# Attention and two expert layers in one kernel: plain loads of q and k with rounding on engines, and another order of batches

## The chip, the cores and the metric

One core of a Trainium2 chip runs the whole program. The time is in microseconds of the device, from the start to the end of one execution. The kernel before had 793.51 us as the median of 3 runs (792.83 to 797.36). One further execution was recorded by the profiler, and all rows below come from it.

## What is computed

Three parts follow each other. Attention over 4 batches of 8 heads, 576 positions, 64 columns a head, with a causal mask and a bias from running sums; then an expert layer that takes the largest of three projections; then an expert layer that sends each of the 2304 tokens to one of 8 experts.

```python
def _attn_ref(q, k, v, s) -> np.ndarray:
    ...
    s_pos = np.maximum(s, 0.0)
    cum = np.cumsum(s_pos, axis=-1)
    bias = -(cum[:, :, :, None] - cum[:, :, None, :])
    scores = np.where(causal, -1000000000.0, scores + np.minimum(bias, 0.0))
    ...
    return np.matmul(attn, v).astype(np.float32)
...
    h = np.maximum(np.maximum(x @ w1, x @ w2), x @ w3)
    return (h @ w_out).astype(np.float32)
...
    e_idx = np.argmax(logits, axis=1)
    ...
        h = np.maximum(x[mask] @ w1[e], 0.0)
        out[mask] = gate_w[mask, None] * (h @ w2[e])
```

## The kernel before

**Precision.** An fp32 value is held as a rounded part of type fp32r ("hi", the names `hl`, `xh`, `w_h`) and what is left of it ("lo", `xl`, `w_l`). A product of two such values takes three matmuls on PE (TensorE): hi by hi, lo by hi, hi by lo. Somebody has to round, and somebody has to subtract.

**Attention.** The 16 pairs of heads `p` are worked through two heads at a time, 32 heads in all. `load(p, j)` brings in a head. Before, it makes three transfers of q and k from memory: SP's queue loads `qk_r` (q in partitions 0 to 63, k in 64 to 127, 288 KB), and POOL's queue loads with a cast to fp32r into `hl` (k's hi of 64x576, 144 KB, L191; q twice, 128x576, 288 KB, L192). Then `k_b`, k's hi once more, comes by a casting load for p < 2 (L194) or from `hl` by a copy on SP's queue, 144 KB. `split` makes the lo parts: k's on DVE into `hl` (L210), q's on POOL into `q_b` (L211). `scores` does two matmuls for each of six blocks (L239, L240), DVE adds the mask and takes the least value (L241), ACT takes the exponential (L243). `inverse` handles the sums (L254), `turned` transposes on PE (L272) with copies on DVE (L275) and ACT (L277), and `values_of` multiplies with v (L295) and writes the result into `x`, scaled by DVE (L296, L297). `load` runs L_AHEAD heads ahead and `split` one head ahead of `scores`.

**Work put between heads.** As soon as all four pairs of a batch are done, projections of the first expert layer for its tokens are put between the heads of later batches (`fill`, with `xh` cast by ACT at L308 and `xl` by POOL at L309): NFILL[b] of the six groups `f`, in pieces of 288 tokens, through PSUM pool `ps_f` and the DRAM array `h_d`. `convert` turns the weights into hi and lo parts (L120 on ACT, L122 and L123 on DVE, L127 on ACT, L128 on POOL); those of `f` < 3 during attention, the fifteen others behind it (`rest`).

**Behind attention.** Six windows of 384 tokens, in the order of the tokens. `stage_a` does the groups `f` that were not done ahead (36 matmuls each, L141 to L143: 4 blocks of 3 for each of three weights), `stage_b` the out-projection of 128 tokens (18 matmuls, L549 to L551), `route` the gating, eight DVE operations a tile (L479) and a ranking on PE (L488). Then the experts run in units of 256 tokens; the weights of the first units are made during the last windows (L591, L592).

**What sets the order.** Each engine works through its list in order. A scheduler that estimates times fixes the lists when the program is built; `issue_after` and `high_priority` bind some instructions to others. SP's and POOL's queues of transfers run in the order of issue.

Of the kernel before, what the change touches and what calls it, by code (L numbers as in the profile page):

```python
# [5 lines left out]
F32 = mybir.dt.float32  # L6
F32R = mybir.dt.float32r
BF16 = mybir.dt.bfloat16
I32 = mybir.dt.int32
ALU = mybir.AluOpType  # L10
# [5 lines left out]
B, H, S, D = 4, 8, 576, 64  # L16
# [6 lines left out]
NP = B * H // 2  # L23
# [29 lines left out]
SENT = 1 << 20  # L53
TABLE = E * STRIDE + UNIT

NFILL = [2, 3, 2, 0]
NPRE = 3
FW = S // 2
FILL_0 = 2
# [7 lines left out]
Z_BUFS = 2  # L67
W1_BUFS = 18
PT_BUFS = 10
L_AHEAD = 4  # L70
FILL_N = [9, 8, 6]
PSB = (3, 3, 1, 1)
HL_BUFS = 4
QR_BUFS = 3
KB_BUFS = 4
QB_N = 3
S_AHEAD = 1
E_N = 4
# [5 lines left out]
def fused_kernel(tc, qk, vd, sd, w64, mod, wg, wgt, mb, we, cst, csi, out):  # L84
    nc = tc.nc
    V, A, G, P, SP = nc.vector, nc.scalar, nc.gpsimd, nc.tensor, nc.sync
    top = ExitStack()
    with top:
# [58 lines left out]
        with ExitStack() as es:  # L147
# [35 lines left out]
            last_load = [None]  # L183


            def load(p, j):
                hl = qkp.tile([128, 2, S], F32R, name="hl", bufs=HL_BUFS)
                x = qkp.tile([128, S], F32, name="qk_r", bufs=QR_BUFS)
                k_b = qkp.tile([66, S], F32R, name="k_b", bufs=KB_BUFS)
                SP.dma_start(out=x, in_=qk[p, :, 0, j])  # L190
                G.dma_start(out=hl[64:128, 0], in_=qk[p, 64:128, 0, j])  # L191
                G.dma_start(out=hl[:, 1], in_=qk[p, :, 1, j])  # L192
                if p < 2:
                    G.dma_start(out=k_b[0:64], in_=qk[p, 64:128, 0, j])  # L194
                if p == 0:
                    A.dma_start(out=k_b.bitcast(F32)[64:66], in_=augk.bitcast(F32)[16 * j:16 * j + 1])
                    if j == 0:
                        SP.dma_start(out=mask[:, S - 128:S], in_=cst[:, 256:384])
                        SP.dma_start(out=ident, in_=cst[:, 0:128])
                else:  # L200
                    if p > 1:
                        SP.dma_start(out=k_b.bitcast(F32)[0:64], in_=hl.bitcast(F32)[64:128, 0])
                    last_load[0] = SP.dma_start(out=k_b.bitcast(F32)[64:66], in_=dk[p, :, j]).ins
                return p, j, hl, x, k_b


            def split(t):
                p, j, hl, x, k_b = t
                q_b = qbs[(2 * p + j) % len(qbs)]
                V.tensor_tensor(out=hl[0:64, 0], in0=x[64:128], in1=hl.bitcast(F32)[64:128, 0], op=ALU.subtract)  # L210
                ins = G.tensor_tensor(out=q_b[0:64], in0=x[0:64], in1=hl.bitcast(F32)[0:64, 1], op=ALU.subtract).ins  # L211
                return ins, (hl, q_b, k_b)

            def values_in(p):
                v_r = vp.tile([128, 5, 128], F32, name="v_r")
                SP.dma_start(out=v_r, in_=vd[p])
                return v_r

            def scores(j, qkb):
# [61 lines left out]


            def values_of(p, v_r, rb, pts):
                b, hp = divmod(p, H // 2)
                if hp == 0:
                    xb[b] = xbp.tile([128, DM // 128, S], F32, tag="xb", name=f"x{b}")
                o_0 = ps_t.tile([128, 512], F32, name="t_ps")
                o_ps = ps_o.tile([128, 512], F32, name="o_ps")

                ins = last_t[0]  # L290
                with tc.high_priority():
                    for o, a0, kb, (i, a, n) in [(o_ps, 512 - t[2], kb, t) for kb, t in enumerate(PV)] + [(o_0, 0, 0, (2, 256, 64))]:
                        for j in (1, 0):
                            with tc.issue_after(ins):
                                ins = P.matmul(o[j * 64:(j + 1) * 64, a0:a0 + n], v_r[:, kb, j * 64:(j + 1) * 64], pts[j][i][:, a:a + n], start=kb == 0, stop=kb == len(PV) - 1 or o is o_0).ins  # L295
                V.tensor_tensor(out=xb[b][:, hp, 64:S], in0=o_ps, in1=rb[:, 128:640], op=ALU.mult)  # L296
                V.tensor_tensor(out=xb[b][:, hp, 0:64], in0=o_0[:, 0:64], in1=rb[:, 64:128], op=ALU.mult)  # L297
# [99 lines left out]
            for p in range(1, NP):  # L397
# [15 lines left out]
                    with tc.issue_after(exps[-1 - CONV_LAG]), tc.issue_after(last_load[0]):  # L413
                        convert(n // 3, n % 3, w0p, "w0", rawp, early=True)
                if p % (H // 2) == H // 2 - 1:
                    b = p // (H // 2)
                    n = 0
                    for i in range(b * S // FW, (b + 1) * S // FW if NFILL[b] else 0):
                        xx, hs = [], {}
                        todo.append((n_head + FILL_0 + n * FILL_N[b] / (6 * NFILL[b]), lambda i=i, xx=xx: xx.extend(fill_x(i, fxp, "fx", V if XL_V else G))))  # L420
                        for f in range(NFILL[b]):
                            for j in range(3):
                                todo.append((n_head + FILL_0 + n * FILL_N[b] / (6 * NFILL[b]), lambda i=i, f=f, j=j, xx=xx, hs=hs: fill(i, f, j, xx, hs, ps_f, fhp, "fh")))
                                n += 1
# [411 lines left out]
def _layout(i):  # L836
# [3 lines left out]
        return a.reshape(NP, 2, S, D).transpose(0, 3, 1, 2)  # L840

    q, k = heads(i["q"]), heads(i["k"])
    qk = np.stack([np.concatenate([q, k], axis=1), np.concatenate([q, q], axis=1)], axis=2)
    v = i["v"].reshape(NP, 2, S, D).transpose(0, 2, 1, 3).reshape(NP, S, 2 * D)
    vd = np.concatenate([v, np.zeros((NP, 64, 2 * D), np.float32)], axis=1).reshape(NP, 5, 128, 2 * D).transpose(0, 2, 1, 3)
    s = i["s"].reshape(NP, 2, S).transpose(1, 0, 2).reshape(2 * NP, S)
# [37 lines left out]
```

## Time and profile before

| | |
|---|---|
| median of 3 runs | 793.51 us |
| profiled execution, its own time | 789.03 us |
| its span | 787.2 us |
| TensorE's mean granted clock | 0.979 |
| PE busy | 722.2 us, 92% |
| DVE busy | 561.1 us, 71% |
| POOL busy | 390.5 us, 50% |
| ACT busy | 361.6 us, 46% |
| DMA read and written | 98.85 and 12.18 MB |

The span is the time between the first and the last instruction that the profiler saw, and the profiled execution's own time holds it. Attention takes the first 285 us, the windows of the first layer end at about 560 us, and the rest are the experts' units. The share of busy time is a mean over these.

### The profile page before, as it was taken

How to read it: one execution, taken by the hardware profiler on the slowest of the kernel's cores; microseconds unless marked ns; L12 is line 12 of the kernel's file. 1: busy time of each engine (PE TensorE's matmuls, PEld its weight loads, DVE VectorE, ACT ScalarE, POOL GpSimd, SP SyncE). 2: the span in 40 equal slices, each digit the busy share in tenths (PEclk: the TensorE clock that was granted, in tenths of full speed). 3: DMA queues.
4: the chain of work that ended last, by engine and by line, in shares of the span. 5: the costliest groups of instructions: out<-in, count | busy, mean ns of one | idle time of the engine just before them, and what ended most of it. 6: DMA issues, size and time to landing. Idle time of an engine off the chain costs nothing. (4 is left out here: it accounts for less than half of the span.)

```text
span 787.2 us, 13802 instructions
## 1 busy us (share of the span) xinstructions
PE 722.2 (92%) x4566; PEld 639.7 (81%) x4566; DVE 561.1 (71%) x1475; ACT 361.6 (46%) x908; POOL 390.5 (50%) x413
## 2 busy tenths in 40 slices
PE   2588699989999995999999999989999999999996
PEld 1566478768988884999989899988998889998884
DVE  5688698879777557876989485983576778666740
ACT  3375456555656444522222222334554655656541
POOL 6544536463433045635263433367456777856641
PEclk9998999999999998999999999999999999999999
DMA  8979768779662156210120101337734766857520
GB/s 196 208 216 229 197 181 200 195 213 247 186 174 80 43 188 193 91 56 21 51 48 17 36 15 52 123 80 219 253 105 164 252 216 242 271 197 251 189 83 18
DMA packets 50706, 118.01 MB, mean 150 GB/s; under 512 B 10497, under 2 KB 14497, under 8 KB 50625
## 3 DMA queue, kind: packets, MB, share of 16 engines
q1 hardware_dynamic: 38216, 90.45, 37.0%
q0 software_dynamic: 12400, 26.57, 13.2%
q8 instruction: 38, 0.62, 0.4%
q14 instruction: 44, 0.35, 0.2%
q10 hardware_dynamic: 8, 0.01, 0.0%
HBM read 98.85 MB, written 12.18 MB: 141 GB/s over the span
## 5 line engine op out<-in xcount | busy, mean ns | idle before, releaser
L141 PE MATMUL a_ps<-xh,w_h 128*128 128x384 f32 (+2 forms) x492 | 159.0, 325 | 3.4 <-DVE h L320 2.9
L142 PE MATMUL a_ps<-xl,w_h 128*128 128x384 f32 (+2 forms) x492 | 158.6, 323 | 0.0
L143 PE MATMUL a_ps<-xh,w_l 128*128 128x384 f32 (+2 forms) x492 | 157.0, 320 | 0.0
L592 DVE TENSOR_TENSOR e_l<-e_raw,e_h 128x512 fp32r<-128x512 f32 x80 | 106.9, 1345 | 43.1 <-ACT e_h L591 40.9
L592 POOL TENSOR_TENSOR e_l<-e_raw,e_h 128x512 fp32r<-128x512 f32 x80 | 109.1, 1383 | 39.4 <-ACT e_h L591 35.0
L243 ACT ACTIVATE e<-e,mn 128x64 f32<-128x64 f32 (+4 forms) x160 | 89.1, 558 | 85.2 <-DVE mn L241 84.8
L479 DVE CUSTOM_DVE_ANT_0 junk<-x,wg 128x512 bf16<-128x512 f32 x120 | 96.4, 804 | 31.8 <-ACT x L553 30.4
L591 ACT CAST e_h<-e_raw 128x512 fp32r<-128x512 f32 x160 | 93.3, 621 | 50.6 <-DMA e_raw<-in_we 38.7
L141 PEld LDWEIGHTS a_ps<-xh,w_h 128*128 128x128 f32 x492 | 93.3, 190 | 5.5 <-DVE h L320 3.7
L142 PEld LDWEIGHTS a_ps<-xl,w_h 128*128 128x128 f32 x492 | 93.6, 190 | 0.9
L143 PEld LDWEIGHTS a_ps<-xh,w_l 128*128 128x128 f32 x492 | 93.5, 190 | 0.5
L239 PE MATMUL s_ps<-hl 128*128 128x64 f32 (+2 forms) x192 | 66.7, 360 | 23.4 <-DMA hl<-in_qk 10.8
L622 PE MATMUL h_ps<-x2t,e_h 128*128 128x256 f32 x288 | 81.0, 286 | 1.1 <-DVE gl L628 1.1
L272 PE MATMUL t_ps<-ident,e 128*128 128x128 f32 x480 | 71.8, 285 | 10.5 <-ACT r_t L259 5.1
L625 PE MATMUL h_ps<-x2t,e_h 128*128 128x256 f32 x288 | 81.0, 283 | 0.0
L626 PE MATMUL h_ps<-x2t,e_l 128*128 128x256 f32 x288 | 80.9, 282 | 0.0
L540 POOL TENSOR_TENSOR fl<-h,fh 128x384 fp32r<-128x384 f32 x36 | 42.8, 1194 | 73.9 <-ACT fh L539 51.7
L241 DVE CUSTOM_DVE_ANT_0 e<-s_ps,mask 128x64 f32<-128x64 f32 (+4 forms) x160 | 64.3, 424 | 9.8 <-PE s_ps L240 9.0
L272 PEld LDWEIGHTS t_ps<-ident,e 128*128 128x128 f32 x480 | 58.4, 146 | 14.6 <-ACT r_t L259 5.4
L239 PEld LDWEIGHTS s_ps<-hl 128*128 128x128 f32 x192 | 39.1, 206 | 30.8 <-DVE mn L241 13.2
L240 PE MATMUL s_ps<-k_b,q_b 66*128 66x64 f32 (+2 forms) x192 | 60.5, 327 | 3.6 <-POOL q_b L211 3.6
L653 PE MATMUL y_ps<-e_h,gh 128*128 128x512 f32 x152 | 61.3, 403 | 0.4 <-ACT gh L645 0.4
(180 smaller groups left out, 1572.5 us busy)
## 6 DMA issues: line engine op xcount, KB each, us to landing
e_raw<-in_we SPq DMA_DIRECT2D x80, 512.0 KB
w_raw<-in_w SPq DMA_DIRECT2D x24, 512.0 KB
qk_r<-in_qk SPq DMA_DIRECT2D x32, 288.0 KB
hl<-in_qk POOLq DMA_DIRECT2D x32, 288.0 KB, 5.1
v_r<-in_vd SPq DMA_DIRECT2D x16, 320.0 KB
rb<-r_d SPq DMA_DIRECT2D x32, 160.0 KB
hl<-in_qk POOLq DMA_DIRECT2D x32, 144.0 KB, 4.0
x2d<-x SPq DMA_DIRECT2D x18, 256.0 KB
```

Source lines behind the costliest of these rows:

```text
L141: P.matmul(a_ps, wh[:, c], xh[:, c], start=c == 0, stop=False)
L142: P.matmul(a_ps, wh[:, c], xl[:, c], start=False, stop=False)
L143: P.matmul(a_ps, wl[:, c], xh[:, c], start=False, stop=c == 3)
L239: P.matmul(s_ps, hl[:, 1, q0:q0 + nq], hl[:, 0, k0:k0 + n], start=True, stop=False)
L243: ex = A.activation(out=ec, in_=ec, func=ACTF.Exp, bias=mn[0:nq, c:c + 1], scale=-1.0, accum_out=l[0:nq, c:c + 1]).ins
L272: last_t[0] = P.transpose(out=t_ps[:, n * 128:(n + 1) * 128], in_=e[:, EOFF[c] + kb * 128:EOFF[c] + (kb + 1) * 128], identity=ident).ins
L479: V.tensor_tensor_reduce(out=junk, in0=x2, in1=wg_sb[ei // 2][:, ei % 2, :], scale=1.0, scalar=0.0, op0=ALU.mult, op1=ALU.add, accum_out=l ...
L591: A.copy(out=h, in_=raw[:, a])
L592: (G if a else V).tensor_tensor(out=lo, in0=raw[:, a], in1=h.bitcast(F32), op=ALU.subtract)
L622: ins = P.matmul(h_ps, w(hs, f, c), xt[:, 0, c], start=c == 0, stop=False).ins
L625: P.matmul(h_ps, w(hs, f, c), xt[:, 1, c], start=False, stop=False)
L626: P.matmul(h_ps, w(ls, f, c), xt[:, 0, c], start=False, stop=c == 3)
```

## The change

Per head one array of 128x2x576 (q twice, then k twice; 576 KB) is loaded plain, by SP alone except at the first head, whose two halves go by SP and ACT. The rounding into `hl` is done by two copies on ACT (64x576 and 128x576), that into `k_b` by a copy on POOL (64x576). The array in memory is laid out for that. Loads run three heads ahead instead of four, with three buffers of `hl` and `k_b` instead of four, and `qk_r` is twice as large. The pairs of heads are taken in the order of batches 1, 2, 3, 0, and the numbers of groups done ahead follow: three for batch 2, two for batches 1 and 3, none for batch 0 (in the diff, of batches 0 to 3).

```diff
--- before.py
+++ after.py
@@ -53,7 +53,9 @@
 SENT = 1 << 20
 TABLE = E * STRIDE + UNIT
 
-NFILL = [2, 3, 2, 0]
+NFILL = [0, 2, 3, 2]
+
+PORD = [(p + H // 2) % NP for p in range(NP)]
 NPRE = 3
 FW = S // 2
 FILL_0 = 2
@@ -67,12 +69,12 @@
 Z_BUFS = 2
 W1_BUFS = 18
 PT_BUFS = 10
-L_AHEAD = 4
-FILL_N = [9, 8, 6]
+L_AHEAD = 3
+FILL_N = [0, 9, 8, 6]
 PSB = (3, 3, 1, 1)
-HL_BUFS = 4
+HL_BUFS = 3
 QR_BUFS = 3
-KB_BUFS = 4
+KB_BUFS = 3
 QB_N = 3
 S_AHEAD = 1
 E_N = 4
@@ -184,36 +186,35 @@
 
 
             def load(p, j):
-                hl = qkp.tile([128, 2, S], F32R, name="hl", bufs=HL_BUFS)
-                x = qkp.tile([128, S], F32, name="qk_r", bufs=QR_BUFS)
+                x = qkp.tile([128, 2, S], F32, name="qk_r", bufs=QR_BUFS)
                 k_b = qkp.tile([66, S], F32R, name="k_b", bufs=KB_BUFS)
-                SP.dma_start(out=x, in_=qk[p, :, 0, j])
-                G.dma_start(out=hl[64:128, 0], in_=qk[p, 64:128, 0, j])
-                G.dma_start(out=hl[:, 1], in_=qk[p, :, 1, j])
-                if p < 2:
-                    G.dma_start(out=k_b[0:64], in_=qk[p, 64:128, 0, j])
+                for t in (range(2) if p == 0 else ()):
+                    (SP, A)[t if j == 0 else 0].dma_start(out=x[:, 1 - t], in_=qk[PORD[p], :, 1 - t, j])
                 if p == 0:
-                    A.dma_start(out=k_b.bitcast(F32)[64:66], in_=augk.bitcast(F32)[16 * j:16 * j + 1])
+                    A.dma_start(out=k_b.bitcast(F32)[64:66], in_=augk.bitcast(F32)[16 * j + PORD[0]:16 * j + PORD[0] + 1])
                     if j == 0:
                         SP.dma_start(out=mask[:, S - 128:S], in_=cst[:, 256:384])
                         SP.dma_start(out=ident, in_=cst[:, 0:128])
                 else:
-                    if p > 1:
-                        SP.dma_start(out=k_b.bitcast(F32)[0:64], in_=hl.bitcast(F32)[64:128, 0])
-                    last_load[0] = SP.dma_start(out=k_b.bitcast(F32)[64:66], in_=dk[p, :, j]).ins
-                return p, j, hl, x, k_b
+                    SP.dma_start(out=x, in_=qk[PORD[p], :, :, j])
+                    last_load[0] = SP.dma_start(out=k_b.bitcast(F32)[64:66], in_=dk[PORD[p], :, j]).ins
+                return p, j, x, k_b
 
 
             def split(t):
-                p, j, hl, x, k_b = t
+                p, j, x, k_b = t
+                hl = qkp.tile([128, 2, S], F32R, name="hl", bufs=HL_BUFS)
                 q_b = qbs[(2 * p + j) % len(qbs)]
-                V.tensor_tensor(out=hl[0:64, 0], in0=x[64:128], in1=hl.bitcast(F32)[64:128, 0], op=ALU.subtract)
-                ins = G.tensor_tensor(out=q_b[0:64], in0=x[0:64], in1=hl.bitcast(F32)[0:64, 1], op=ALU.subtract).ins
+                A.copy(out=hl[64:128, 0], in_=x[64:128, 1])
+                A.copy(out=hl[:, 1], in_=x[:, 0])
+                G.tensor_copy(out=k_b[0:64], in_=x[0:64, 1])
+                V.tensor_tensor(out=hl[0:64, 0], in0=x[64:128, 1], in1=hl.bitcast(F32)[64:128, 0], op=ALU.subtract)
+                ins = G.tensor_tensor(out=q_b[0:64], in0=x[0:64, 0], in1=hl.bitcast(F32)[0:64, 1], op=ALU.subtract).ins
                 return ins, (hl, q_b, k_b)
 
             def values_in(p):
                 v_r = vp.tile([128, 5, 128], F32, name="v_r")
-                SP.dma_start(out=v_r, in_=vd[p])
+                SP.dma_start(out=v_r, in_=vd[PORD[p]])
                 return v_r
 
             def scores(j, qkb):
@@ -281,7 +282,7 @@
 
 
             def values_of(p, v_r, rb, pts):
-                b, hp = divmod(p, H // 2)
+                b, hp = divmod(PORD[p], H // 2)
                 if hp == 0:
                     xb[b] = xbp.tile([128, DM // 128, S], F32, tag="xb", name=f"x{b}")
                 o_0 = ps_t.tile([128, 512], F32, name="t_ps")
@@ -413,7 +414,7 @@
                     with tc.issue_after(exps[-1 - CONV_LAG]), tc.issue_after(last_load[0]):
                         convert(n // 3, n % 3, w0p, "w0", rawp, early=True)
                 if p % (H // 2) == H // 2 - 1:
-                    b = p // (H // 2)
+                    b = PORD[p] // (H // 2)
                     n = 0
                     for i in range(b * S // FW, (b + 1) * S // FW if NFILL[b] else 0):
                         xx, hs = [], {}
@@ -840,7 +841,7 @@
         return a.reshape(NP, 2, S, D).transpose(0, 3, 1, 2)
 
     q, k = heads(i["q"]), heads(i["k"])
-    qk = np.stack([np.concatenate([q, k], axis=1), np.concatenate([q, q], axis=1)], axis=2)
+    qk = np.stack([np.concatenate([q, q], axis=1), np.concatenate([k, k], axis=1)], axis=2)
     v = i["v"].reshape(NP, 2, S, D).transpose(0, 2, 1, 3).reshape(NP, S, 2 * D)
     vd = np.concatenate([v, np.zeros((NP, 64, 2 * D), np.float32)], axis=1).reshape(NP, 5, 128, 2 * D).transpose(0, 2, 1, 3)
     s = i["s"].reshape(NP, 2, S).transpose(1, 0, 2).reshape(2 * NP, S)
```

ACT's list at the start of the program; `hl_168`, `hl_189` and `hl_230` of the changed kernel are the first three heads' arrays, `e0_132` the first head's exponentials. Before:

```order
L181 ACTIVATE q_b0_129<-s3_85 2x576
L181 ACTIVATE q_b1_130<-s3_85 2x576
L181 ACTIVATE q_b2_131<-s3_85 2x576
L196 DMA k_b_161<-augk_86 2x1x576
L196 DMA k_b_175<-augk_86 2x1x576
L243 ACTIVATE e0_132,l_210<-e0_132,mn_209 128x64
L243 ACTIVATE e0_132,l_210<-e0_132,mn_209 128x192
```

And in the changed kernel:

```order
L209 CAST hl_168<-qk_r_159 128x576
L208 CAST hl_168<-qk_r_159 64x576
L194 DMA k_b_160<-augk_86 2x1x576
L194 DMA k_b_175<-augk_86 2x1x576
L208 CAST hl_189<-qk_r_174 64x576
L209 CAST hl_189<-qk_r_174 128x576
L208 CAST hl_230<-qk_r_181 64x576
L209 CAST hl_230<-qk_r_181 128x576
L244 ACTIVATE e0_132,l_196<-e0_132,mn_195 128x64
```

Six casts, those of the heads 0, 1 and 2, now stand ahead of the first exponential.

PE's list behind attention, before: the last filling matmuls (128x288), then out-projections (L549) of the first two tiles' group `fh0`, and then the next projections of 384 tokens.

```order
L143 MATMUL a_ps_3541<-xh_3310,w_l_1265 128x288
L549 MATMUL b_ps_4083<-w_h_3799,fh0_3793 128x512
L549 MATMUL b_ps_4143<-w_h_3799,fh0_3793 128x512
L141 MATMUL a_ps_3943<-xh_3682,w_h_3716 128x384
L142 MATMUL a_ps_3943<-xl_3683,w_h_3716 128x384
L143 MATMUL a_ps_3943<-xh_3682,w_l_3717 128x384
```

In the changed kernel the first out-projection (L550) stands behind all 216 projections of window 0, of which these are the last three:

```order
L143 MATMUL a_ps_4121<-xh_3684,w_h_3784 128x384
L144 MATMUL a_ps_4121<-xl_3685,w_h_3784 128x384
L145 MATMUL a_ps_4121<-xh_3684,w_l_3785 128x384
L550 MATMUL b_ps_4167<-w_h_3842,fh0_3836 128x512
L551 MATMUL b_ps_4167<-w_l_3843,fh0_3836 128x512
L552 MATMUL b_ps_4167<-w_h_3842,fl0_3837 128x512
```

The projections moved ahead of the first out-projection, and the lines of the changed kernel are one or two numbers higher there.

## Rows read from the trace of the kernel before

**Rows 1.** Windows: length, busy PE, PEld, DVE, ACT, POOL (instructions), clock, DMA share, GB/s

```profile
0.00:43.00 43.00, 19.57 (x84) 16.06 (x85) 25.74 (x79) 16.64 (x48) 25.23 (x62) 1.00 0.88 203
43.00:111.00 68.00, 56.53 (x368) 42.07 (x369) 55.50 (x156) 36.45 (x111) 31.05 (x42) 0.87 0.79 208
111.00:284.00 173.00, 165.08 (x1261) 141.70 (x1257) 130.95 (x408) 99.94 (x302) 69.89 (x88) 0.99 0.61 162
...
305.00:313.00 8.00, 0.27 (x3) 0.05 (x1) 6.86 (x10) 4.03 (x9) 4.97 (x4) 0.79 0.72 216
313.00:340.00 27.00, 27.00 (x143) 25.40 (x144) 18.46 (x23) 11.94 (x27) 18.54 (x19) 0.93 0.26 88
340.00:560.00 220.00, 216.64 (x1233) 201.67 (x1232) 169.49 (x563) 65.72 (x157) 97.64 (x87) 1.00 0.26 78
```

**Rows 2.** Waits of PE, 0 to 43 us: total, times, longest

```profile
PE s_ps L239 <- DMA hl<-in_qk: 10.8, 1, 10.8
PE s_ps L239 <- DVE mn L241: 5.7, 4, 3.4
```

**Rows 3.** Timeline of DVE (start, length): last reduction of heads 0 to 3

```profile
17.70 0.51 DVE L241 CUSTOM_DVE_ANT_0 e<-s_ps,mask,mn 128x288 f32<-128x288 f32 x1
...
31.41 0.51 DVE L241 CUSTOM_DVE_ANT_0 e<-s_ps,mask,mn 128x288 f32<-128x288 f32 x1
...
35.39 0.52 DVE L241 CUSTOM_DVE_ANT_0 e<-s_ps,mask,mn 128x288 f32<-128x288 f32 x1
...
42.18 0.51 DVE L241 CUSTOM_DVE_ANT_0 e<-s_ps,mask,mn 128x288 f32<-128x288 f32 x1
```

**Rows 4.** Lines by shape, ACT's casts, 40 to 284 us: busy, mean ns

```profile
L308 ACT CAST xh<-x 128x288 fp32r<-128x288 f32 x24 | 8.9, 428 | 4.3 <-DVE x L297 2.6 <-PE a_ps L142 1.7
...
L514 ACT CAST xh<-x 128x384 fp32r<-128x384 f32 x4 | 1.8, 510 | 0.7 <-issue 0.7
```

**Rows 5.** Lines by shape, POOL, 0 to 284 us

```profile
L211 POOL TENSOR_TENSOR q_b<-qk_r,hl 64x576 fp32r<-64x576 f32 x32 | 46.3, 1447 | 15.2 <-PE s_ps L240 6.0 <-DMA hl<-in_qk 5.1 <-issue 1.9
...
L192 POOL DMA_DIRECT2D hl<-in_qk x32 | 18.5, 579 | 0.6 <-DMA k_b<-in_qk 0.6
```

**Rows 6.** Timeline of POOL, a copy with a cast

```profile
11.14 0.29 POOL L368 CAST tri<-tri_f 128x128 bf16<-128x128 f32 x1 [5.28 <-DMA iota<-in_cst]
```

**Rows 7.** Timeline, one DVE operation beside POOL's subtraction and without

```profile
89.51 1.97 DVE L254 TENSOR_SCALAR r<-l 128x8 f32<-128x8 f32 x1
...
90.63 0.81 POOL L309 TENSOR_TENSOR xl<-x,xh 128x288 fp32r<-128x288 f32 x1
...
269.50 0.17 DVE L254 TENSOR_SCALAR r<-l 128x8 f32<-128x8 f32 x1
```

**Rows 8.** Timeline of ACT, in brackets the idle time before

```profile
97.38 0.66 ACT L120 ACTIVATE w_z<-w_raw 128x512 f32<-128x512 f32 x1 [6.73 <-DMA w_raw<-in_w]
```

**Rows 9.** Waits of PE, 284 to 340 us

```profile
PE b_ps L549 <- ACT w_h L127: 7.7, 1, 7.7
PE a_ps L141 <- DVE h L320: 1.6, 1, 1.6
```

**Rows 10.** Timeline behind attention: DVE's last product, matmul pitches, last weight

```profile
284.49 0.68 DVE L296 TENSOR_TENSOR x<-o_ps,rb 128x512 f32<-128x512 f32 x1
...
303.60 0.30 PE L142 MATMUL a_ps<-xl,w_h 128*128 128x288 f32 x1
...
304.93 0.29 PE L143 MATMUL a_ps<-xh,w_l 128*128 128x288 f32 x1
...
318.98 0.33 PE L142 MATMUL a_ps<-xl,w_h 128*128 128x384 f32 x1
...
320.37 0.33 PE L141 MATMUL a_ps<-xh,w_h 128*128 128x384 f32 x1
...
331.75 1.29 POOL L128 TENSOR_TENSOR w_l<-w_z,w_h 128x512 fp32r<-128x512 f32 x1
```

**Rows 11.** Lines, DVE, 340 to 560 us

```profile
L479 DVE CUSTOM_DVE_ANT_0 junk<-x,wg 128x512 bf16<-128x512 f32 x120 | 96.4, 804 | 31.8 <-ACT x L553 30.4
```

## Prediction

> **What bounds the kernel now.** I read the table of windows first, since the share of busy time says nothing about single stages [rows 1]. From 111 us on TensorE is busy 165.08 of 173 us, later 216.64 of 220. There only less matmul work would help, and the change removes none. Three stretches are different. From 0 to 43 us, the first four heads, PE is busy 19.57 us and the DMA engines 0.88 of the time. From 43 to 111 us PE is busy 56.53 of 68 at a mean clock of 0.87, DMA still at 0.79. From 305 to 313 us, between attention and the first out-projection, PE does 0.27 us of work. About 23 + 11 + 8 us of idle PE lie in these three, and the change touches all of them.
>
> Next PE's waits in the first 43 us: one of 10.8 us for the first casting load of q, then four for DVE, 5.7 us together [rows 2]. The DVE rows give the pace. The last reduction of heads 0, 1, 2 and 3 starts at 17.70, 31.41, 35.39 and 42.18 us [rows 3]. Where nothing is late a head costs 35.39 − 31.41 = 4.0 us; between heads 0 and 1 there are 13.7 us, between 2 and 3 6.8. Heads 1 and 3 stood for their loads: a head loads 864 KB (288 + 288 + 144 + 144 of q, k and their rounded copies), four heads 3.5 MB, and at 203 GB/s [rows 1] that alone is 17 us, to which come values, mask and tables.
>
> **The change, part by part.** All terms are on the profiled execution, 789.03 us; the median of the runs shown, 793.51, is 4.48 us above it, and I add that at the end.
>
> (a) *Startup.* A head now loads 576 KB. Ahead of head 2's scores stand three heads and a value tile, 3 × 576 + 320 KB plus 0.2 MB of tables, about 2.3 MB or 11 to 12 us at 203 GB/s, after a first 1.5 us; so head 2's data is there at about 13 us, before head 0 is through. ACT has the casts of heads 1 and 2 in its queue ahead of head 0's first exponential, but the reductions that set the pace are DVE's and don't wait for it. Head 0 then ends near 17 us as before, heads 1, 2, 3 follow at 4.0 to 4.4 us, so head 3 ends at 29.4 to 31 us against 42.7. The gain is 11.7 to 13.3, less some 2 us of transposes of head 0 and 1 that PE and DVE did in the gaps of before: **−10.5** (−13 to −6; the weak end is heads at 5.5 us).
>
> (b) *Traffic from 43 to 111 us.* At 0.79 a third of a head's q and k bytes fall away. ACT stands 6.73 us for one weight tile that is late [rows 8], and PE has 11.5 us idle and loses clock. I take half of the idle time: **−6** (−10 to −2; 10 is nearly all of it).
>
> (c) *ACT's casts.* Two per head, 576 columns each, of 64 and 128 partitions. The casts of 288 and 384 columns took 428 and 510 ns [rows 4], or 0.85 ns a column on top of 0.18 us: 0.68 us for 576, 1.35 us a head, 43 us in all, and 38 us for the 28 heads that (a) does not hold. ACT is busy 99.94 of 173 us in 111 to 284 [rows 1], where 20 heads run: 3.65 us idle a head. The 1.35 us fit in, but ACT takes its instructions in order, and an exponential behind a cast comes up to 0.68 us later. If that hits the path in about a quarter of the heads, it is 0.18 us a head: **+5**. The ends are 0 (all covered by those 3.65 us) and 20 (half of the casts exposed).
>
> (d) *POOL.* A copy of 64x576 from one operand. No row shows it: the 128x128 cast took 0.29 us [rows 6], the subtraction of 64x576 with two operands 1.45 [rows 5]. I take 0.9, between them. Two issues of casting loads, 0.58 us each, go [rows 5], so POOL's time per head falls a little. But POOL at tensor work holds up DVE: the same 128x8 operation took 1.97 us, to 91.48, beside a POOL subtraction that ended at 91.44, and 0.17 without [rows 7]. The new copy starts when the load lands; DVE's subtraction of the same head waits for ACT's cast, 0.68 us later, so it meets only the last 0.2 us of the copy. I take 0.1 us a head: **+3** (0 to +8).
>
> The Trainium skill speaks against this move: "SBUF — State Buffer", section "SBUF: two separate sides", says that GpSimd and a DVE operation with two SBUF inputs or in its fast mode lock one port pair for a whole instruction, the other blocking. The rows at 89.51 agree [rows 7]. By this rule taken at its worst, each of 28 copies stopping DVE for its whole 0.9 us, term (d) would be +25 and the sum +6.
>
> (e) *End of attention.* Batch 0 comes last and has no projections ahead of time, so window 0 has six groups of projections to do before its first out-projection instead of four: 2 × 36 matmuls of 384 columns at 0.174 us (from 318.98 to 320.37 are eight) are 12.5 us of work pulled into the gap; 14 fewer filling matmuls of 288 at 0.133 take 1.9 out [rows 10]. 10.6 us of cover stand against 7.7 + 1.6 us of waits [rows 9] and 0.07 × 27 = 1.9 us of lost clock after them [rows 1]. What is late next is the weights: the last of fifteen conversions ended at 333.04, 48.5 us after attention's last product at 284.49 [rows 10], and PE now arrives at 48 × 0.133 + 216 × 0.174 = 44 us plus the first tile's earlier out-projections, about 47. Some 2 us remain: **−9** (−11 to −5).
>
> (f) *The last windows.* The moved groups are missing at the end: windows 4 and 5 have 3.5 and 4 of them instead of 5 and 6, each 36 × 0.174 = 6.3 us. DVE's gating, 3 × 8 instructions of 804 ns a window or 19 us [rows 11], and the first experts' weights have that much less cover. **+1.5** (0 to +6, one group's length).
>
> Sum: −10.5 − 6 + 5 + 3 − 9 + 1.5 = −16, so 789.03 − 16 = 773.0, and with 4.48 a median of 777.5.
>
> **Rivals.**
> *ACT paces attention.* If a cast on ACT delays every head by 0.5 us, (c) is +14 instead of +5 and the median 786.5. For it: exponentials, copies of the transposed scores and casts stand in one in-order queue. Against: 3.65 us idle a head.
> *The casts lie wholly on the path (slower).* DVE's subtraction waits for ACT's cast, POOL's for the second; if ACT reaches them only after the exponentials of the head before, each head carries 1.35 us: 28 × 1.35 = 38, sum +17, median 810.5. It decides from 0.75 us a head, where 28 × 0.75 = 21 eats the gain of 16 and the 5 taken. For it: one head of split-ahead and loads three heads ahead instead of four. Against: PE is what was full in that stretch, and a head's casts may be done any time in the head before.
> *DVE stopped by the copies for their whole length.* (d) at +25 and a median of 799.5; the page on SBUF would have it so at its worst. Against: DVE works mostly on PSUM with one SBUF operand there, and POOL's other subtractions already run beside it.
> *The weights stay the bound.* If fifteen conversions end later because ACT and POOL have more to do, (e) is −1: median 785.5.
> *The startup's gain is not kept.* Heads come earlier but weights and filling work not: (a) −5 and (b) −2 instead of −16.5 leave 787.
> *The tail is late.* (f) +6: 782.
>
> **How the numbers follow.** Chances: the forecast, 768 to 785, 0.46; the tail 0.09; ACT pacing 0.14; the gain not kept 0.10; the weights 0.07; DVE stopped 0.04; casts on the path 0.06; all terms at their good ends, under 768, 0.04. About 1% (7.9 us) is what a measurement can tell here, so faster means under 785.6, slower over 801.4. Faster is 0.46 + 0.09 + 0.04 + half of the weights and a part of the rest, 0.68; slower is casts on the path and part of DVE stopped, 0.09; the rest 0.23 is within 1%. From 765 to 792 leaves out casts on the path, DVE stopped, the far end of ACT pacing and half of the good ends: less than 0.2.
>
> **What would show it.** (a) Head 3's last reduction at 30 to 31 us, no 10 us gap after head 0. (b) DMA share from the same head on well under 0.79 and no stop of ACT for a weight tile. (c) Casts of 0.6 to 0.8 us and PE waits for ACT or for the subtractions during attention not above 5 us more. (d) A copy near 0.9 us, DVE's 64x576 subtraction still near its length of before. (e) A wait of about 2 us at the first out-projection instead of 7.7, on a weight. (f) PE waits under 2 us more in windows 4 and 5. The prediction is wrong if heads take over 0.75 us longer from head 12 on, or if attention ends early and the first out-projection doesn't.

## The result, and the profile after it

The changed kernel took 773.3 us in the median (770.4 to 774.8, 4 runs), the kernel before 795.4 beside it; the ratio is 0.9735 with a 95% interval of 0.970 to 0.977. The prediction was 777.5 with a range of 765 to 792, so the time and the sign came out. The terms behind it did not all: attention gained more than was forecast, and the end lost more.

Windows of the changed kernel's profile (the columns are those of [rows 1]; attention ends at 268 us, the first out-projection is done at 324):

```profile
0.00:43.00 43.00, 28.09 (x144) 22.67 (x145) 34.31 (x104) 32.99 (x87) 22.29 (x53) 1.00 0.63 188
43.00:111.00 68.00, 59.64 (x419) 46.71 (x419) 61.06 (x175) 50.45 (x138) 34.67 (x37) 0.97 0.62 191
111.00:268.00 157.00, 152.10 (x1166) 131.47 (x1163) 117.76 (x365) 107.81 (x301) 57.43 (x65) 0.99 0.43 130
268.00:289.00 21.00, 19.84 (x124) 19.61 (x124) 13.69 (x25) 8.25 (x15) 8.40 (x6) 1.00 0.69 235
289.00:324.00 35.00, 35.00 (x200) 33.54 (x199) 24.40 (x32) 16.20 (x34) 23.38 (x22) 1.00 0.30 99
...
460.00:560.00 100.00, 90.54 (x506) 81.05 (x504) 75.21 (x238) 43.06 (x93) 57.93 (x49) 0.94 0.53 165
560.00:772.00 212.00, 199.14 (x1255) 177.81 (x1253) 125.20 (x175) 108.56 (x222) 124.27 (x100) 0.97 0.50 176
```

PE's work in the first 43 us rose from 19.57 to 28.09 us and DMA's share fell from 0.88 to 0.63; the hole of 8 us behind attention is gone. But from 460 us on PE, which had hardly waited in these stages before, is idle for 9.5 of 100 us, and its clock is below 1.00.

DVE's last reduction of heads 0 to 3, as in [rows 3], and the last large product of attention, as in [rows 10]:

```profile
16.55 0.50 DVE L242 CUSTOM_DVE_ANT_0 e<-s_ps,mask,mn 128x288 f32<-128x288 f32 x1
...
22.17 0.51 DVE L242 CUSTOM_DVE_ANT_0 e<-s_ps,mask,mn 128x288 f32<-128x288 f32 x1
...
25.93 0.52 DVE L242 CUSTOM_DVE_ANT_0 e<-s_ps,mask,mn 128x288 f32<-128x288 f32 x1
...
31.71 0.52 DVE L242 CUSTOM_DVE_ANT_0 e<-s_ps,mask,mn 128x288 f32<-128x288 f32 x1
...
268.36 0.68 DVE L297 TENSOR_TENSOR x<-o_ps,rb 128x512 f32<-128x512 f32 x1
```

From these and the times of the same events before, the 15.2 us between the spans (787.2 and 772.0) divide so:

| stretch | before to after | difference |
|---|---|---|
| start to head 3's last reduction | 42.18, 31.71 | −10.5 |
| from there to attention's last product | 242.3, 236.6 | −5.7, with 2.5 us more filling work in it, so −8.2 |
| to the first two tiles' copies | 54.6, 54.3 | −0.2, with 12.5 us more projections and 2.5 us less filling work in it, so −10.2 |
| to the last matmul's end | 441.4, 436.9 | −4.5, with 12.5 us fewer projections, so +8.0 |
| to the end of the span | 6.8, 12.5 | +5.7 |

The 12.5 us are the prediction's own 2 × 36 × 0.174 [rows 10]. The 2.5 us are 19 filling matmuls at 0.133 [rows 10]: in the change 463 of all 504 start ahead of attention's last product, before it were 444. The medians lie 22.1 us apart, not 15.2, since the profiled execution before took 789.0 us, less than each of the four runs above (792.8 to 800.8), and that of the change 773.8, close to its median; the other 7 us can't be placed by the table.

The copies behind the first out-projections are these rows, of before and of the changed kernel:

```profile
339.05 1.08 ACT L553 COPY x<-b_ps 128x512 f32<-128x512 f32 x2 [4.83 <-PE b_ps L551]
```

```profile
322.69 1.08 ACT L554 COPY x<-b_ps 128x512 f32<-128x512 f32 x2
```

The new operations, grouped by line and shape from 0 to 284 us; the number behind the bar and comma is the mean in ns:

```profile
L209 ACT CAST hl<-qk_r 128x576 fp32r<-128x576 f32 x32 | 21.5, 673 | 0.8
L208 ACT CAST hl<-qk_r 64x576 fp32r<-64x576 f32 x32 | 21.4, 669 | 13.3 <-issue 9.7 <-PE s_ps L240 2.9
...
L210 POOL CAST k_b<-qk_r 64x576 fp32r<-64x576 f32 x32 | 23.1, 723 | 61.9 <-PE s_ps L241 38.3 <-PE s_ps L240 13.0 <-issue 3.7
...
L211 DVE TENSOR_TENSOR hl<-qk_r,hl 64x576 fp32r<-64x576 f32 x32 | 34.9, 1090 | 5.5 <-ACT hl L208 4.6
```

ACT's casts took 0.67 us, as worked out from [rows 4]. POOL's copy took 0.72, where 0.9 was taken. DVE's subtraction of 64x576 had a mean of 1.09 us, where it had 0.79 before, but it is not POOL's copy that holds it. In 11 of the 32 heads it began while POOL's subtraction for `q_b` was running, and ended 0.62 us behind that; in the other 21 it took 0.75. The copy held it in none: in the two heads where the copy had begun first, it was over within 0.05 us of the subtraction's start. One of the 11, DVE's row and POOL's:

```profile
27.98 1.82 DVE L211 TENSOR_TENSOR hl<-qk_r,hl 64x576 fp32r<-64x576 f32 x1
```

```profile
27.78 1.40 POOL L212 TENSOR_TENSOR q_b<-qk_r,hl 64x576 fp32r<-64x576 f32 x1
```

Both now wait for ACT's casts, which follow each other, and this is probably why they meet more often than before, where DVE's was held in 3 heads. Over all of DVE's operations in attention, what each took above the shortest of its kind beside POOL's work adds up to some 25 us before and 23 in the change, 0.7 of it beside the copy (an estimate from the two traces).

One caution for all that follows: executions of the same list of instructions differ. Three of the kernels below have the changed kernel's lists word for word through attention, and theirs ended at 2 us less to 4 us more. And a kernel that is built anew with one more instruction in each head gets new lists from the scheduler; where pieces of filling work moved, the comparison counts them out at the 0.133 us of [rows 10]. The time of the last product of values of the pair, less 0.133 us for each filling matmul before it, is then:

| kernel | 4th pair | 7th | 9th | 16th |
|---|---|---|---|---|
| before | 87 | 129 | 152 | 225 |
| changed | 79 | 112 | 137 | 207 |
| loads only | 79 | 113 | 138 | 208 |
| order only | 89 | 126 | 149 | 222 |
| ACT's extra copies | 94 | 135 | 159 | 229 |
| extra load | 79 | 128 | 149 | 222 |
| POOL's extra copy | 83 | 121 | 149 | 229 |
| k's cast on POOL | 87 | 126 | 152 | 237 |
| casting load of k_b | 80 | 113 | 141 | 208 |

The gain of attention is made by the seventh pair (17 us) and then kept, neither growing nor shrinking by more than 2, which is within what two executions of the same lists differ by.

### The profile page after: what moved, and what is told of

The parts are those of the page before. It is cut to its first block, busy times and chain, and to the rows that moved or that the text cites. A ratio compares the mean times of both kernels' runs of the same rounds, so it can differ in the third digit from the quotient of the medians.

```text
span 772.0 us, 13710 instructions
## 1 busy us (share of the span) xinstructions
PE 720.3 (93%) x4566; PEld 639.8 (83%) x4566; DVE 554.6 (72%) x1475; ACT 400.2 (52%) x972; POOL 380.7 (49%) x377
## 4 chain that ended last, share of the span: by engine, by line
PE 68%; DVE 11%; DMA 8%; issue 6%; ACT 3%; POOL 1%; SPq 0%; ACTq 0%; POOLq 0%; DVEq 0%
PE a_ps L143 7%; PE a_ps L144 7%; PE a_ps L145 7%; PE h_ps L626 5%; PE h_ps L623 5%; PE h_ps L627 5%; PE y_ps L654 4%; PE y_ps L656 4%; PE y_ps L655 4%; DMA w_raw<-in_w 4%; PE t_ps L273 3%; PE o_ps L296 3%; PE b_ps L550 3%; PE b_ps L551 3%; PE b_ps L552 3%
## 5 line engine op out<-in xcount | busy, mean ns | idle before, releaser
L480 DVE CUSTOM_DVE_ANT_0 junk<-x,wg 128x512 bf16<-128x512 f32 x120 | 93.1, 776 | 30.3 <-ACT x L554 29.0
L541 POOL TENSOR_TENSOR fl<-h,fh 128x384 fp32r<-128x384 f32 x36 | 44.7, 1246 | 78.4 <-ACT fh L540 60.4
L273 PE MATMUL t_ps<-ident,e 128*128 128x128 f32 x480 | 69.7, 279 | 6.3 <-DVE pt L276 2.7
L273 PEld LDWEIGHTS t_ps<-ident,e 128*128 128x128 f32 x480 | 56.8, 144 | 10.1 <-DVE pt L276 4.1
L212 POOL TENSOR_TENSOR q_b<-qk_r,hl 64x576 fp32r<-64x576 f32 x32 | 48.0, 1500 | 30.3 <-ACT hl L209 27.9
```

The lines of the kernel that those rows point to most:

```text
L273: last_t[0] = P.transpose(out=t_ps[:, n * 128:(n + 1) * 128], in_=e[:, EOFF[c] + kb * 128:EOFF[c] + (kb + 1) * 128], identity=ident).ins
L480: V.tensor_tensor_reduce(out=junk, in0=x2, in1=wg_sb[ei // 2][:, ei % 2, :], scale=1.0, scalar=0.0, op0=ALU.mult, op1=ALU.add, accum_out=l ...
```

## Experiments

### The two halves apart

The loads alone: the changed kernel with the old order.

```diff
-NFILL = [0, 2, 3, 2]
+NFILL = [2, 3, 2, 0]
-PORD = [(p + H // 2) % NP for p in range(NP)]
+PORD = list(range(NP))
-FILL_N = [0, 9, 8, 6]
+FILL_N = [9, 8, 6]
```

> The changed kernel with the batches in the old order 0, 1, 2, 3 and the old numbers of projections done ahead. Theory: the loads shorten attention by themselves, by the 16 us that the last product of attention came earlier in the profile of the change (266.8 against 282.9 us), and the stages behind are those of before: about 778 us where before has 794. Rival, the terms (a) to (d) of the prediction as they stood: -8.5, about 786. Second rival: the gain needs the new order, 792 to 796.

Measured: 778.0 us, ratio 0.977 (0.971 to 0.984). The order alone, the kernel before with PORD in every address and the new numbers:

```diff
-NFILL = [2, 3, 2, 0]
+NFILL = [0, 2, 3, 2]
+PORD = [(p + H // 2) % NP for p in range(NP)]
```

> The kernel before with the batches in the order 1, 2, 3, 0 and the new numbers of projections done ahead; casting loads as before. Theory: about 12 us gained where attention ends (no wait of 7.7 us at the first out-projection), of which some 8 are lost again in the last windows and at the first expert units, because windows 4 and 5 have 3.5 us and 2 groups less to cover DVE's gating: about 789 us where before has 794, with waits for the ranking of tiles 13 or 14. Rival, terms (e) and (f) of the prediction as they stood: -9 and +1.5, about 786. Second rival: the order is worth nothing, 794.

Measured: 788.4 us, ratio 0.992 (0.988 to 0.996). The two ratios multiply to 0.970, and both together had 0.9735: the halves add up within their intervals. The waits of PE behind attention say where each acts. The loads alone, 265 to 345 us, keep the hole:

```profile
PE a_ps L143 <- ACT h L534: 8.3, 1, 8.3
PE b_ps L552 <- POOL fl L541: 1.8, 1, 1.8
```

With the order alone it is gone (waits of 1.2 and 0.9 us from 284 to 340), but the waits at the end are there, from 460 to 580:

```profile
PE rk L490 <- DVE oh L459: 3.4, 1, 3.4
PE x_ps L606 <- DMA xg<-x2d,mt: 3.1, 2, 2.9
```

So the order takes the hole away and brings the late ranking, and attention's gain comes with the loads (207 against 208 in the table's last column).

### Are ACT's casts covered?

```diff
                 A.copy(out=hl[:, 1], in_=x[:, 0])
+                A.copy(out=scr, in_=x[:, 1, 0:448])
+                A.copy(out=scr, in_=x[:, 0, 0:448])
```

> The changed kernel with two more copies of 128x448 on ACT in every head, into a scratch array that nobody reads: about 1.1 us more of ACT per head, 36 us in all. Theory: ACT's casts lie in its idle time, so 36 us more cost at most 4: 773 to 777 us where the change has 773. Rival, ACT paces the heads: 0.5 us or more a head, 789 us and above; with all of it on the path 809.

Measured: 800.9 us, 27.6 more than the change, with 64 more copies of 0.56 us on ACT, whose busy time rose by 31 us. The rival stood, and not as a cost per head: by the table 15 us are lost by the fourth pair, 23 by the seventh and 22 at the end. The windows show why:

```profile
0.00:43.00 43.00, 27.60 (x119) 21.32 (x121) 33.29 (x104) 37.37 (x97) 20.69 (x50) 1.00 0.56 162
43.00:111.00 68.00, 51.94 (x323) 38.91 (x320) 59.97 (x150) 54.53 (x143) 32.47 (x36) 0.82 0.61 185
111.00:290.00 179.00, 170.30 (x1282) 145.85 (x1281) 119.70 (x386) 128.45 (x347) 59.62 (x68) 0.97 0.41 124
```

ACT is busy 37.4 of the first 43 us, and from 43 to 111 PE has less to do and a mean clock of 0.82, where the change had 0.97; 0.15 × 68 is 10 us, if PE bounds all of that stretch. The first four heads were still on time; this is head 3's last reduction, which started at 31.71 in the change:

```profile
31.65 0.52 DVE L245 CUSTOM_DVE_ANT_0 e<-s_ps,mask,mn 128x288 f32<-128x288 f32 x1
```

Behind the seventh pair, where filling work keeps PE full, ACT's extra copies cost nothing. So ACT with this much more work paces the heads from the fifth to about the fourteenth, and not the rest. The lists are new ones, and what part of the 22 us they made is not told apart.

### Are the bytes what counts?

```diff
+                SP.dma_start(out=scr, in_=qk[PORD[p], :, 0, j, 0:448])
                 return p, j, x, k_b
```

> The changed kernel with one more plain load of 128x448, 224 KB, in every head into a scratch array that nobody reads: 800 KB a head instead of 576 (864 before). Theory: the bytes set the pace of the first heads, so four heads take 0.9 MB at 203 GB/s or 4.4 us longer and some 3 us more go up to 111 us: about 781 us where the change has 773, head 4's first score 4 us later. Rival: the gain came from leaving POOL's casting queue, not from bytes: 773 to 775.

Measured: 787.1 us, 13.8 more than the change, but not where it was expected. Head 3's last reduction and the fourth pair (79) are as early as in the change, with more bytes moved:

```profile
31.64 0.51 DVE L244 CUSTOM_DVE_ANT_0 e<-s_ps,mask,mn 128x288 f32<-128x288 f32 x1
```

```profile
0.00:43.00 43.00, 29.09 (x157) 24.25 (x158) 34.45 (x111) 33.52 (x89) 23.79 (x54) 1.00 0.79 242
```

242 GB/s at a DMA share of 0.79 are 306 at a full one; the kernel before had 203 at 0.88, or 231. So at 800 KB a head plain loads still kept up, and the 864 KB with two casting transfers among them did not: DMA time per byte was a third higher there. The loss came later, in one piece, at 124 us, where ACT stood for a weight:

```profile
135.35 0.66 ACT L122 ACTIVATE w_z<-w_raw 128x512 f32<-128x512 f32 x1 [11.09 <-DMA w_raw<-in_w]
```

It is the stop of [rows 8] once more. This run can't say that the bytes did it: the added load writes one array again and again, and SP's queue waited 17.7 us from 100 to 140 for the one before to land, with the weight behind it. What it does show is the mechanism of term (b): a late weight on SP's queue stops ACT, and with it PE.

### POOL's copy

```diff
                 G.tensor_copy(out=k_b[0:64], in_=x[0:64, 1])
+                G.tensor_copy(out=scr[0:64], in_=x[0:64, 1, 0:448])
```

> The changed kernel with one more copy of 64x448 on POOL in every head, into a scratch array that nobody reads: about 0.56 us a head by the 0.72 us that the copy of 64x576 took, 18 us in all. Theory: POOL has the time, and its copies hold up DVE only where the two meet (DVE's 64x576 subtraction took 1.09 us in the changed kernel, 0.79 before): 0.1 us a head, 776 us where the change has 773. Rival: each copy stops DVE for its whole length, 0.56 us a head, 785 to 791.

Measured: 821.7 us, 48 more. Both expectations were too low. By the table 22 us of it lie in attention; the rest is mostly filling work that the new lists no longer put between the heads: 113 matmuls start behind attention's last product (41 in the change), and PE waits between their pieces. From 297 to 329 us PE does 84 of them; the row shows the 28 of one line, with 10.7 us of idle time before them:

```profile
L143 PE MATMUL a_ps<-xh,w_h 128*128 128x288 f32 x28 | 11.5, 411 | 10.7 <-DVE h L323 6.2 <-ACT h L321 2.5 <-ACT xh L311 2.0
```

The next run takes work off ACT and puts it on POOL:

```diff
-                A.copy(out=hl[64:128, 0], in_=x[64:128, 1])
+                G.tensor_copy(out=hl[64:128, 0], in_=x[64:128, 1])
```

> The changed kernel with the first of the two casts, k's 64x576, made by POOL instead of ACT: 0.67 us a head less on ACT, 0.72 more on POOL. Theory: ACT paces the first heads (36 us more of ACT had cost 27.6), so 21 us less give back 5 to 12: 761 to 768 us where the change has 773. Rival: POOL's copy stands in the way of DVE's subtraction and is itself behind POOL's other work, so the heads get no faster: 773 to 780.

Measured: 839.5 us, 66 more, 30 of them in attention. In both runs POOL's first copy of a head waited for the load itself, 30.1 and 26.4 us in all up to 284 us; the rows are POOL's waits of the one run and of the other:

```profile
POOL k_b L211 <- DMA qk_r<-in_qk: 30.1, 11, 4.2
```

```profile
POOL hl L208 <- DMA qk_r<-in_qk: 26.4, 8, 8.1
```

In the change it waited 2.5 us for it:

```profile
POOL k_b L210 <- DMA qk_r<-in_qk: 2.5, 3, 1.3
```

The loads are late because SP issues them in order behind loads that wait for a buffer: in the run with the extra copy the sixth head's load of q and k was issued at 28.1 us, in the change at 17.5. How much of the 22 and 30 us POOL's own slowness made and how much the new order of SP's queue, these two runs don't tell apart; they do show that another 0.6 us a head on POOL is not free with the lists that come with it.

The last of this kind replaces POOL's copy by a casting load.

```diff
-                G.tensor_copy(out=k_b[0:64], in_=x[0:64, 1])
+                G.dma_start(out=k_b[0:64], in_=qk[PORD[p], 0:64, 1, j])
```

> The changed kernel with k_b filled by a casting load of 144 KB from memory on POOL's queue in every head instead of POOL's copy: 720 KB a head. Theory: by the 13.8 us that 224 KB more a head had cost, 144 KB cost up to 9, and DVE's subtraction falls from 1.09 to 0.8 us, up to 9 us back: 771 to 780 us where the change has 773. The stretch from the last matmul to the end was 12.2 to 12.4 us with the plain loads and 6.8 and 7.1 with the casting ones: if it goes with the casting loads on POOL's queue it is 7 here; rival: it goes with the rest of the program, 12.

Measured: 784.0 us. Attention ends as in the change (208 against 207), with 144 KB more a head, and DVE's subtraction is hardly shorter (1.03 us): without the copy POOL's subtraction for `q_b` holds it still. The loss is mostly behind attention, and 4 us of it lie behind the last matmul: 16.4 us to the end, neither 7 nor 12, told below.

### The end of the windows

```diff
-T_PE = NT - MW // 128
+T_PE = NT - 2 * (MW // 128)
-            if t < T_PE:
+            if t < NT - MW // 128:
                 route(t, x2)
```

> The changed kernel with the gating of tiles 12 to 14 by transposes and matmuls on PE, as it is for tiles 15 to 17 already, instead of eight DVE operations a tile. Theory: DVE's gating bounds the last two windows since they have fewer projections; with 19 us less on DVE the wait of 3.6 us for the ranking, that of 3.0 us for the gathered rows and the slower clock behind them go: 766 to 769 us where the change has 773. Rival: the waits come from the weights of the first units, which stay: 773, or 775 with PE's 3 us more of work.

Measured: 774.2 us, no change. The wait for the ranking went, and others came in its place, with PE's own transposes besides (460 to 560 us):

```profile
PE lg_ps L478 <- ACT x2t_r L474: 3.2, 2, 2.5
PE x_ps L605 <- DMA xg<-x2d,mt: 2.2, 2, 1.9
```

The same stretch in the change:

```profile
PE rk L489 <- DVE oh L458: 3.6, 1, 3.6
PE x_ps L605 <- DMA xg<-x2d,mt: 3.0, 1, 3.0
```

Then the subtractions for the first unit's weights, all on POOL, and all on DVE:

```diff
-(G if a else V).tensor_tensor(out=lo, ...
+(G if a or n == 0 else V).tensor_tensor(out=lo, ...
```

> The changed kernel with all sixteen subtractions for the weights of the first expert unit on POOL, instead of eight on DVE: some 9 us less on DVE in windows 4 and 5 and at no cost on PE. Theory: DVE, with gating and these subtractions, bounds the last windows (the ranking of one tile came 3.6 us late): 767 to 770 us where the change has 773. Rival: the weights then come later from POOL and the first unit waits for them: 773 to 780.

Measured: 782.1 us. Less work on DVE made DVE later:

```profile
PE rk L489 <- DVE oh L458: 8.1, 3, 4.2
```

The timeline of that run shows one of the three, DVE's row and POOL's:

```profile
506.70 2.72 DVE L458 TENSOR_SCALAR oh<-iota,ix 128x8 bf16<-128x8 f32 x1
...
506.90 2.49 POOL L593 TENSOR_TENSOR e_l<-e_raw,e_h 128x512 fp32r<-128x512 f32 x2
```

An operation on eight columns stood for as long as POOL's two subtractions ran, to 509.4 us. In the change the same operation took this, twice in a row:

```profile
490.39 0.22 DVE L458 TENSOR_SCALAR oh<-iota,ix 128x8 bf16<-128x8 f32 x1
...
505.56 0.22 DVE L458 TENSOR_SCALAR oh<-iota,ix 128x8 bf16<-128x8 f32 x1
```

The other way:

```diff
-(G if a else V).tensor_tensor(out=lo, ...
+(G if a and n else V).tensor_tensor(out=lo, ...
```

> The changed kernel with all sixteen subtractions for the weights of the first expert unit on DVE, none on POOL: the opposite of the run that put them all on POOL and took 9 us more. Theory: what makes the gating of tiles 12 to 14 late is not the amount of DVE's work but that its operations stand still while POOL subtracts (a 128x8 operation of 0.15 to 0.22 us took up to 1.6 us there in the change, up to 2.7 with all sixteen on POOL). Eight subtractions at 0.68 us more on DVE, 5.5 us, free it of eight holds of up to 1.3: 768 to 772 us where the change has 773, the waits for the ranking under 2 us. Rival: DVE's amount of work bounds: the ranking gets later, 776 to 780.

Measured: 775.3 us (771.5 to 779.9), ratio 0.973 (0.968 to 0.978): the same as the change. From tile 12's copy to the first unit's last projection the profiles have 59.5 us, against 61.9 in the change and 68.6 with all on POOL, so the direction is the theory's, with 9 us between the ends. But the 2.4 us don't reach the end. A ranking is still 3.2 us late inside that stretch, and behind it the experts' units take 3.2 us longer than in the change (the profile is of the execution of 779.9 us). DVE's holds by POOL are one cause of the late gating; that they are the whole of the 8 us is not shown.

More cover for the last windows, by other numbers of projections done ahead:

```diff
-NFILL = [0, 2, 3, 2]
+NFILL = [0, 3, 3, 1]
-FILL_N = [0, 9, 8, 6]
+FILL_N = [0, 16, 8, 3]
-CONV = {..., 5: [5], 7: [6], 8: [7], 9: [8]}
+CONV = {..., 5: [5], 6: [6], 7: [7, 8]}
```

> The changed kernel with three groups of projections done ahead for batches 1 and 2 and one for batch 3, instead of 2, 3 and 2 (batch 1's pieces spread over more heads, and the last weights of the third group converted a pair earlier). Windows 4 and 5 then have 4 and 5 groups instead of 3.5 and 4. Theory: the last windows lose 8 us because they are short; a group and a half more in them hides 4 to 8 of these: 766 to 770 us where the change has 773. Rival: the pieces no longer fit between the heads (in PE's list 86 filling matmuls stand behind attention's last product, 50 in the change), and at 0.133 to 0.37 us each the 36 more take back 5 to 13: 773 to 780.

Measured: 796.4 us, 23 more than the change. The filling pieces fell out of attention, as the rival had it, and the first out-projection's copies came at 337 us. The last windows were not helped: PE waited 5.8 and 4.9 us for rankings there, with longer windows. So longer windows alone don't bring the rankings in time; which work of DVE and POOL made them late under these new lists is not taken apart.

### The look-ahead

```diff
-KB_BUFS = 3
+KB_BUFS = 4
-PT_BUFS = 10
+PT_BUFS = 9
```

> The changed kernel with four buffers of k_b instead of three (and nine of the transposed scores instead of ten, for room). The change waited 17.5 us in the first 111 on SP's queue at the load of k_b's last two rows, for a buffer that PE still read, with the load of q and k behind it. Theory: that wait holds up the next head's data only where ACT or POOL wait for them, which in the change they did for under 3 us: 771 to 774 us where the change has 773. Rival: the look-ahead of the loads, cut from four buffers to three, holds the heads: 763 to 768.

Measured: 782.4 us, slower than both expectations. The lists differ from the start, and PE waited 9.1 us for DVE's reductions from 43 to 111, 6.1 of them at once. Whether the buffers or the lists made it is open; nothing speaks for the look-ahead holding the change.

## Why the prediction was right, and where it wasn't

**(a) Startup, −10.5: right in size.** Head 3's last reduction came 10.5 us earlier, at 31.71 where 29.4 to 31 was said. The reason was not. Bytes over 203 GB/s was the working, but with 800 KB a head in plain loads this reduction is as early (31.64), at 242 GB/s. So what the runs leave is that q and k for `hl` come by plain loads, which take less DMA time per byte; that the smaller number of bytes helped is not shown. What limits the first four heads now is open: neither 224 KB more a head, nor a casting load of `k_b` (31.30), nor two more copies a head on ACT (31.65) delayed them.

**(b), (c), (d), −6 + 5 + 3 = +2: measured −8.2.** From head 3 to attention's end the change gained. The weight that had stopped ACT for 6.73 us [rows 8] stops it for 1.2 at most up to 111 us, and the clock from 43 to 111 rose from 0.87 to 0.97, which is at most 0.10 × 68 = 6.8 us. Of the +8 for ACT and POOL nothing shows behind the ninth pair. For ACT the run with extra copies gives the reason: they cost nothing where PE is full, and much before. So 0.18 us a head, spread evenly, was the wrong shape; what the casts themselves cost in the first seven pairs is inside (a) and (b), and no run takes it out. For POOL, the 0.1 us a head was to come from its copy, and the copy never held DVE's subtraction; what DVE lost beside POOL's work in attention did not grow. "SBUF — State Buffer" of the Trainium skill, section "SBUF: two separate sides", has a GpSimd instruction and such a DVE operation shut each other out. The trace agrees, and the one that had begun first went on: DVE's subtraction took up to 1.98 us instead of 0.75 where POOL's had begun before it, and POOL's up to 1.83 instead of 1.40 where DVE's had. As a price of the change, 0.9 us a head as worked from it at its worst, it did not come.

**(e) End of attention, −9: measured −10.2.** The hole, the short wait and the lost clock, 7.7 + 1.6 + 1.9 = 11.2, all went, and the two microseconds kept for the last weight were not needed: PE never waited for a weight there, only 1.2 us for a copy of ACT. The order alone gave −9.0 in this stretch.

**(f) The last windows, +1.5: measured +8.0, beyond the bound of 6.** This is the term that failed. Of the 8.0, 0.7 lie ahead of tile 12's copy, 5.7 from there to the first unit's last projection, and the rest in the experts' units; the order alone gave 0.6, 6.1 and 1.1. Less cover was the right mechanism, but it was sized by one group's length at most. PE works in order, and a ranking that is late by 3.6 us stops everything behind it, after which the clock is lower: 0.89 from 500 to 530 us. Before, with longer windows, these waits were there but short (480 to 580 us):

```profile
PE rk L488 <- DVE oh L457: 2.2, 2, 1.1
PE x_ps L604 <- DMA xg<-x2d,mt: 1.2, 1, 1.2
```

DVE's gating is late in part because its operations stand still beside POOL's subtractions. The rows for that were there before [rows 7], and the prediction used them for attention only. The holds themselves are not new; one of them before:

```profile
514.44 1.83 DVE L456 CUSTOM_DVE_ANT_0 lt<-lt,iota 128x8 f32<-128x8 f32 x1
```

Counted as above, they come to some 20 us in either kernel, from tile 9's copy to the first unit's last projection. What went is the cover over them; that this is the whole of the 8 us is not shown.

**Not in the sum: +5.7** from the last matmul to the end of the span, below.

So −8.5 for attention was −18.7, −7.5 for the rest was −2.2, and 5.7 came unseen: −16 against −15.2. That the total came out is luck, since the errors had both signs. The median then lay 4.2 us below the forecast because the 4.48 us between profile and median before were added, and the change's profiled execution was only 0.5 above its median. Of the rivals, the one of the late tail was right as a mechanism, with 8 us instead of 6; ACT pacing attention showed only with more work on ACT than the change gives it, and not behind the seventh pair.

## What to carry to other kernels

Price a moved operation by stage: work added to ACT was free here where PE was full, and costly where ACT itself was nearly full. When work is pulled forward, look at what it had been covering, and at every in-order engine there on which a late small operation stops the large ones behind it. Before adding POOL work beside DVE work, look in the trace for DVE operations with a duration far from their usual one, and see which of the two engines had begun first.

## What the runs showed of the hardware that was not expected

**The end of the program goes with the transfers that POOL issued.** POOL's last scatter starts 1.1 us behind the last matmul in every kernel. In the kernel before:

```profile
781.50 0.99 POOL L658 DMA_INDIRECT out<-y,mt  x1 [6.33 <-ACT y L657]
```

In the changed kernel, and the page's row of POOL's queue (packets, MB, share):

```profile
760.64 0.97 POOL L659 DMA_INDIRECT out<-y,mt  x1 [6.37 <-ACT y L658]
```

```profile
q0 software_dynamic: 4912, 11.82, 4.8%
```

With the casting load of k_b:

```profile
766.32 0.98 POOL L659 DMA_INDIRECT out<-y,mt  x1 [6.33 <-ACT y L658]
```

```profile
span 781.7 us, 13715 instructions
...
q0 software_dynamic: 7472, 16.54, 7.6%
```

From the scatter's start to the end of the span are 5.7 us before (787.2), 11.4 in the change (772.0) and 15.4 with the casting load (781.7). Nearly all of the difference is in two of POOL's closing instructions: its drain took 1.05, 5.38 and 7.99 us, the one ahead of it 0.43, 1.50 and 2.14. The drain was the same to 0.01 us in every kernel with the same number of POOL's transfers (133 before and with the order alone, 65 in the change and the ten others with plain loads alone, 97 here). For 65 and 97 transfers that is 0.083 and 0.082 us each, but 133 took 1.05 in all, so what it hangs on is open. It came with the new loads, and the 5.7 us took back part of the 18.7 that attention gained.

**What POOL holds up and what not.** DVE's gating products (128x512, both operands in memory on the chip, L480) took 0.68 us in the 83 cases of the change without POOL's tensor work beside them and 0.98 in the mean of the 37 with it: 14 of these took 0.97 to 2.64, the others 0.68 as well. The reductions of the scores, with one operand in PSUM, had the same mean, 0.44 us over all shapes, beside POOL's work and without it.
